# Batch 1's k and q by another queue, cast on chip, and turned six blocks a piece

## The chip, the cores and the metric

The kernel runs on one core of one Trainium2 chip. Its engines are TensorE (PE), VectorE (DVE), ScalarE (ACT), GpSimd (POOL) and SyncE (SP). PE multiplies, and turns blocks of data by a multiplication with an identity matrix; DVE, ACT and POOL work on elements; SP only issues DMAs. ACT and POOL issue DMAs too. A DMA that POOL issues can change the type on its way (fp32 in memory, bf16 on chip); one that SP issues here cannot. The two kinds run in different queues on the same 16 DMA engines: in the profile POOL's are the queue q0, "software_dynamic", and SP's are q1, "hardware_dynamic".

The metric is the device time in microseconds (us) of one execution; the median of several runs is compared.

## What is computed

Chunked attention over 4 batches, 8 heads, 768 positions of 64 elements, with 8 memory rows for each head, and then a feed-forward layer with a sine in it, over all 3072 positions:

```python
for c in range(S // 32):                       # chunks of 32 queries
    l, r = max(0, 32*c - 16), min(S, 32*c + 40)
    k_full = concat([mem_k, k[:, :, l:r]]); v_full = concat([mem_v, v[:, :, l:r]])
    a = softmax(q[:, :, 32*c:32*c + 32] @ k_full.T / sqrt(64))
    out[:, :, 32*c:32*c + 32] = a @ v_full
x = out.transpose(0, 2, 1, 3).reshape(3072, 512)
h = x @ w_in                                   # 512 x 2048
g = h + sin(alpha * h)**2 / (alpha + 1e-9)
return g @ w_out                               # 2048 x 512
```

## The kernel before

**The stages.** The work runs as a front and four passes. The front makes the attention of batch 0. Pass i makes the feed-forward layer of batch i, and, woven into it, the attention of batch i+1. The order of everything is written out by hand as strings of words, one letter and some digits each, and a method `do_<letter>` issues what a word stands for. Each engine works off its own instructions strictly in that order, so a word that waits holds up what stands behind it on the same engine.

**The feed-forward words.** The inner size 2048 is cut into 16 tiles. `b7` and `h7` multiply the two halves of tile 7 (four matmuls each, line 424) and let ACT take the sine (line 439); `q7A`, `q7V` or `q7P` square it on ACT, DVE or POOL (lines 444 and 447); `g7` makes the tile of gT on DVE from it (line 451) and frees the PSUM banks. `f9` issues nine matmuls of the second product (line 462), which has its own queue of waiting work; finished rows are copied by ACT or DVE (line 469) and written by SP (line 472).

**The attention words.** Batches 0 and 1 get their turned k and q from PE. `k2` turns piece 2 of k (a piece is a pair of heads) and `l2` piece 2 of q (`turn`, line 269); `K2V`, `L2A` copy the result out of PSUM on DVE or ACT (lines 285, 291 and 299) into kT and qT. `s61` makes the scores of blocks 6 and 1 (lines 385 and 399) and needs all pieces; `v0` multiplies block 0 by the values (line 414); `T0`, `t1`, `c6` turn the result into the next batch's x. Batches 2 and 3 get their turned k and q from DMA transposes and are not touched by the change.

**The loads.** `I7g` loads the columns of w_in for tiles 7 to 15, `I27` those for tiles 2 to 6 (line 213); `U12` loads one block of rows of w_out (line 219); `V125` loads v of batch 1, heads 2 to 4 (lines 172 and 179, two DMAs). All are POOL's, and cast on their way. At most eight of POOL's DMAs are under way: the ninth waits until the first has landed.

For batch 0 SP loads k and q in fp32, a piece at a time, into `kq_f` (line 708), and words like `a4V` cast a piece on ACT or DVE (`do_a`, line 653) into `k_bf` or `q_bf`. For batch 1 two words in pass 0, `dq108` and `dk108`, let POOL load all of q and all of k at once, cast by the DMA (`load_one`, line 155).

**The layout.** `k_bf` and `q_bf` hold 128 rows of `(head, r, d)`, with r from 0 to 5 and d from 0 to 63. A block of one head is 64 columns wide, so `turn` makes 12 transposes a piece: six for each of the two heads, the first head's into rows 0 to 63 of PSUM and the second head's into rows 64 to 127.

**gT.** The pool that holds gT has two buffers that passes use in turn.

In pass 0 the words around the pieces of batch 1 stand in this order (others left out):

```
b0 h0 I7g U69 U12 b1 h1 dq108 b4 h4 b3 h3 b6 dk108 b2 h2 h6 b5 h5 Ufg b7 U01 U56 q6P h7 U24 q7P U45 ... V158 ...
l0 l2 l3 q13P k2 Ube U9b Uef ... V125 k1 k0 l1 K1V k3 L1V L3A q14V K3A K0A V102 f9 g14 s61
```

Of the kernel before, what the change touches and what calls it, by code (L numbers as in the profile page):

```python
# [9 lines left out]
P = 128  # L10
# [4 lines left out]
BF = mybir.dt.bfloat16  # L15
F32 = mybir.dt.float32
ACTF = mybir.ActivationFunctionType
ALU = mybir.AluOpType


class Feed:
# [64 lines left out]
def kernel(  # L86
# [12 lines left out]
    nc = tc.nc  # L99
    B, H, S, D = q.shape  # L100
# [4 lines left out]
    HP = H // 2  # L105
    FT = d_ff // P
    KT = d_model // P
    NSUB = S // P
# [14 lines left out]
    ident = consts.tile([P, P], BF, name="ident")  # L123
# [17 lines left out]
    qst = q_bf[:].rearrange("p h r d -> p (h r d)").rearrange("p (t c) -> p t c", t=NSUB)  # L141
# [8 lines left out]
    inv_alpha = consts.tile([P, FT], F32, name="inv_alpha")  # L150

    def load_one(src, dst, b, h0, h1):
        nc.gpsimd.dma_start(
            dst[:, h0:h1].rearrange("p h r d -> p h (r d)"),
            src[b, h0:h1].rearrange("h (p r) d -> p h (r d)", p=P),
        )

    def load_v(b, h0, h1):  # L160
        vw = vws[b % 2][:].rearrange("p h j c -> p (h j) c")
# [107 lines left out]
    def turn(src, hp):  # L269
        bank, bs = banks.single()  # L270
        t = bank[:, 0:384].bitcast(BF).rearrange("p (r c) -> p r c", r=6)
        for r in range(6):
            for e in range(2):
                nc.tensor.transpose(
                    t[64 * e:64 * e + 64, r, :], src[:, 2 * hp + e, r, :], ident[:]
                )
# [73 lines left out]
    def normed(otv, bs):  # L350
# [5 lines left out]
            in1=rinv[:].unsqueeze(3).to_broadcast([QW, 2, HP, D]),  # L356
            op=ALU.mult,
        )
# [82 lines left out]
    def squared(t, eng):  # L441
# [3 lines left out]
        else:  # L445
            e = nc.vector if eng == "V" else nc.gpsimd
            e.tensor_tensor(out=s2[:], in0=u[:], in1=u[:], op=ALU.mult)  # L447

    def finish(t, gT):
# [53 lines left out]
    class Stage:  # L503
# [146 lines left out]
        def do_a(self, a):  # L650
            hp = int(a[0]) % HP
            dst = kq[int(a[0]) // HP]
            copier(a[1])(
                dst[:, 2 * hp:2 * hp + 2].rearrange("p h r d -> p h (r d)"), kq_f[int(a[0])][:]
            )

        def do_C(self, a):
            consts_of[a]()
# [4 lines left out]
        def do_d(self, a):  # L663
            if a == "m":
                nc.gpsimd.dma_start(memv_st[64:72].rearrange("n b h d -> n (b h) d"),
                                    mem_v.rearrange("b h n d -> n (b h) d"))
            elif a == "y":
                for bb in range(1, B):
                    if CROSSED[bb][0]:
                        nc.gpsimd.dma_start(  # L670
                            memv_st[96:104, bb],
                            mem_k[bb].rearrange("h n d -> n h d"))
            else:
                src, dst = (k, k_bf) if a[0] == "k" else (q, q_bf)
                load_one(src, dst, int(a[1]), int(a[2]), int(a[3]))

        def do_I(self, a):
            load_w_in(P * int(a[0], 17), P * int(a[1], 17))
# [21 lines left out]

    kq_f = [mlp.tile([P, 2, 6 * D], F32, name="kq_f", tag=t) for t in ("u", "s2") * 4]
    memk_f = mlp.tile([P, H, D], F32, name="memk_f", tag="o_sb", bufs=3)
    alpha_rows = mlp.tile([FT, P], F32, name="alpha_rows", tag="o_sb", bufs=3)

    def load_f(src, hp, t):
        nc.sync.dma_start(
            t[:], src[0, 2 * hp:2 * hp + 2].rearrange("h (p r) d -> p h (r d)", p=P)
        )  # L710

    load_f(k, 0, kq_f[0])
# [90 lines left out]
    def const_s():  # L803
# [6 lines left out]
    first = {}  # L810
    stage = Stage(-1, None)
    stage.tile = first
    stage.run((
# [3 lines left out]
    ))  # L817
    for i, words in enumerate(((
# [6 lines left out]
    ),(  # L825
# [5 lines left out]
    ),(  # L831
# [5 lines left out]
    ),(  # L837
# [3 lines left out]
    ))):  # L841
        stage = Stage(i, stage.nx).run(words)
    feed.take(400)

# [28 lines left out]
```

## Time and profile before

| | |
|---|---|
| median of 3 runs | 216.53 us (216.51 to 219.29) |
| span of the profiled execution, first to last instruction | 213.1 us |
| what the median has beyond that span | 3.4 us |
| PE busy | 201.7 us, 95% of the span |
| ACT, DVE, POOL busy | 143.5, 140.5, 99.8 us |
| granted TensorE clock | 1.000 throughout |
| read from memory, written | 29.66 MB, 6.29 MB |

The profiled execution's own time is not listed apart from its span; sums over the trace are made against the span, and 3.4 us are added to compare with the median. In the rows of a timeline the columns are start, length, engine, line, operation, destination and source, count, and in brackets the idle time before it and what ended that; PEq, SPq and the like are queues that issue. A row may join several instructions that follow each other.

### The profile page before, as it was taken

The numbers are of one execution on the slowest core, as the hardware profiler recorded it, in microseconds if no ns is written. First come the engines' busy times: TensorE is split into PE (matmuls) and PEld (weight loads), VectorE is DVE, ScalarE is ACT, GpSimd is POOL, SyncE is SP. The second block draws the span as 40 slices with busy tenths as digits, with TensorE's granted clock in tenths as the row PEclk, the third lists the DMA queues.
The fourth block names the chain that finished last, engine by engine and source line by source line (L and its number), as shares of the span: only waits on it lengthen the run. The fifth ranks groups of instructions, "written<-read, shape, count | busy, mean of one in ns | idle before, by whom it ended". The sixth has DMA issues, their size and how long they took to land.

```text
span 213.1 us, 4479 instructions
## 1 busy us (share of the span) xinstructions
PE 201.7 (95%) x1721; PEld 113.5 (53%) x1721; DVE 140.5 (66%) x218; ACT 143.5 (67%) x230; POOL 99.8 (47%) x140
## 2 busy tenths in 40 slices
PE   0799899999999999999999999999999999999994
PEld 0456555565455556555455555554555555554443
DVE  7598678999542749975856649898157197865011
ACT  2597898976857469977846199887846289891110
POOL 8959515688598193009991039659400023200000
PEclk9999999999999999999999999999999999999999
DMA  6999999999999999969999229989945400000312
GB/s 195 337 163 141 193 209 205 204 163 182 131 177 141 137 148 144 180 88 110 126 217 171 72 63 131 156 126 129 175 115 123 124 15 0 2 3 0 148 49 98
DMA packets 95908, 28.19 MB, mean 132 GB/s; under 512 B 84864, under 2 KB 92432, under 8 KB 95888
## 3 DMA queue, kind: packets, MB, share of 16 engines
q0 software_dynamic: 68736, 13.25, 92.3%
q1 hardware_dynamic: 26976, 14.62, 28.2%
q8 instruction: 13, 0.21, 0.4%
q14 instruction: 7, 0.06, 0.1%
q10 hardware_dynamic: 176, 0.04, 0.1%
HBM read 29.66 MB, written 6.29 MB: 169 GB/s over the span
## 4 chain that ended last, share of the span: by engine, by line
PE 71%; DVE 9%; DMA 7%; ACT 4%; issue 4%; POOL 3%; DVEq 0%; POOLq 0%; ACTq 0%
PE ps L462 38%; PE ps L424 27%; DMA memv_st<-in_mem_v_dram 4%; DVE gT L451 4%; DVE s L447 3%; DMA vw<-in_v_dram 3%; PE ps L414 3%; PE ps L385 2%; ACT u L439 2%; PE ps L366 1%; ACT s L444 1%; POOL s L447 1%; POOL vw L172 1%; DVE kT L285 1%; ACT L699 1%
## 5 line engine op out<-in xcount | busy, mean ns | idle before, releaser
L462 PE MATMUL ps<-w_out_sb,gT 128*128 128x512 bf16 (+2 forms) x400 | 89.1, 371 | 0.0
L424 PE MATMUL ps<-xT,w_in_sb 128*128 128x384 bf16 x512 | 86.0, 326 | 0.7 <-DVE gT L451 0.4
L451 DVE SCALAR_TENSOR_TENSOR gT<-s,inv_alpha,ps 128x768 bf16<-128x768 f32 x64 | 63.0, 1011 | 12.5 <-ACT s L444 5.2
L424 PEld LDWEIGHTS <-w_in_sb 128*128 128x128 bf16 x512 | 49.8, 98 | 35.4 <-issue 2.1
L439 ACT ACTIVATE u<-ps,alpha_sb 128x768 f32<-128x768 f32 x64 | 56.6, 895 | 16.8 <-PE ps L424 14.3
L462 PEld LDWEIGHTS <-gT 128*128 128x128 bf16 x400 | 36.6, 98 | 37.9 <-DVE gT L451 0.2
L447 POOL TENSOR_TENSOR s<-u 128x768 f32<-128x768 f32 x11 | 17.4, 1582 | 69.7 <-ACT u L439 69.7
L399 ACT ACTIVATE pt<-ps,biasm 128x256 bf16<-128x256 f32 x72 | 27.2, 489 | 10.5 <-PE ps L385 10.5
L469 DVE COPY o_sb<-ps 128x512 f32<-128x512 f32 (+1 forms) x15 | 10.1, 678 | 28.3 <-PE ps L462 26.4
L447 DVE TENSOR_TENSOR s<-u 128x768 f32<-128x768 f32 x23 | 21.9, 953 | 7.8 <-ACT u L439 7.8
L444 ACT ACTIVATE s<-u 128x768 f32<-128x768 f32 x30 | 25.0, 841 | 0.5
L354 DVE TENSOR_TENSOR x_blk<-ps,rinv 96x512 bf16<-96x512 f32 x32 | 22.0, 687 | 1.1
L469 ACT COPY o_sb<-ps 128x512 f32<-128x512 f32 (+1 forms) x10 | 5.6, 562 | 21.6 <-PE ps L462 21.6
L172 POOL DMA_DIRECT2D vw<-in_v_dram x13 | 12.9, 994 | 7.9 <-PE ps L366 5.4
L353 DVE RECIPROCAL rinv<-ps 96x8 f32<-96x8 f32 x32 | 6.4, 200 | 13.5 <-PE ps L414 12.7
L179 POOL DMA_DIRECT2D vw<-in_v_dram x13 | 12.7, 976 | 0.0
L238 POOL DMA_DIRECT2D kst<-in_k_dram x16 | 12.2, 760 | 1.1 <-DMA vw<-in_v_dram 0.8
L232 POOL DMA_DIRECT2D kst<-in_k_dram x16 | 11.3, 708 | 2.3 <-DMA vw<-in_v_dram 1.6
L369 ACT COPY xT<-ps 128x384 bf16<-128x384 bf16 x12 | 5.6, 496 | 8.2 <-PE ps L366 8.2
L245 POOL DMA_DIRECT2D q_bf<-in_q_dram x12 | 10.7, 912 | 0.0
L414 PEld LDWEIGHTS <-pt 128*128 128x128 bf16 x192 | 8.2, 97 | 4.2 <-ACT pt L399 0.3
L414 PE MATMUL ps<-vw,pt 128*128 128x65 bf16 x192 | 8.9, 193 | 0.0
(81 smaller groups left out, 131.4 us busy)
## 6 DMA issues: line engine op xcount, KB each, us to landing
out_dram<-o_sb SPq DMA_DIRECT2D x23, 256.0 KB, 2.3
kq_f<-in_k_dram SPq DMA_DIRECT2D x4, 384.0 KB, 6.5
kq_f<-in_q_dram SPq DMA_DIRECT2D x4, 384.0 KB, 6.0
q_bf<-in_q_dram POOLq DMA_DIRECT2D x12, 128.0 KB, 6.7
w_in_sb<-in_moe_w_in_dram POOLq DMA_DIRECT2D x1, 1152.0 KB, 12.6
vw<-in_v_dram POOLq DMA_DIRECT2D x7, 128.0 KB, 6.7
vw<-in_v_dram POOLq DMA_DIRECT2D x8, 112.0 KB, 7.4
kst<-in_k_dram POOLq DMA_DIRECT2D x14, 64.0 KB, 5.1
```

Of the source, the lines that this page charges most:

```text
L172: nc.gpsimd.dma_start(vw[0:64, lo:c1, 0:D], win(vflat, a, n, 64))
L179: nc.gpsimd.dma_start(vw[72:128, c0:hi, 0:D], win(vflat, base + QW * c0 + 48, hi - c0, 56))
L354: nc.vector.tensor_tensor(out=x_blk[:].rearrange("p g e d -> p e g d"), in0=otv[0:QW, :, :, 0:D], in1=rinv[:].unsqueeze(3).to_broadcast([Q ...
L399: nc.scalar.activation(pt[:, 0:H * QW].rearrange("p (g e c) -> p g e c", g=2, e=4)[:, :, :, 32 * m:32 * m + 32], sc[:, :, 0:4 * QW].rearra ...
L414: nc.tensor.matmul(otv[:, e, hp, :], pt[:, QW * i:QW * i + P], vws[b % 2][:, 2 * hp + e, j, 0:D + 1],)
L424: nc.tensor.matmul(t["hT"][:, hf, 0:HALF], w_in_sb[:, kt, P * t["ft"]:P * t["ft"] + P], t["xT"][:, kt, HALF * hf:HALF * hf + HALF], start= ...
L439: nc.scalar.activation(t["u"][:], t["hT"][:, :, 0:HALF], ACTF.Sin, scale=alpha_sb[:, ft:ft + 1])
L444: nc.scalar.activation(s2[:], u[:], ACTF.Square)
L447: e.tensor_tensor(out=s2[:], in0=u[:], in1=u[:], op=ALU.mult)
L451: nc.vector.scalar_tensor_tensor(out=gT[:, ft, :].rearrange("p (e c) -> p e c", e=2), in0=t["s2"][:], scalar=inv_alpha[:, ft:ft + 1], in1= ...
L462: nc.tensor.matmul(o[:, c0:c1], gT[:, ft, P * s:P * s + P], w_out_sb[:, ft, c0:c1], start=(ft == 0), stop=(ft == FT - 1),)
L469: copier(state["engines"][state["o"] % len(state["engines"])])(o_sb[:, c0:c1], o[:, c0:c1])
```

## The change

For batch 1, k and q are loaded by SP in fp32, in eight DMAs of one piece each, as batch 0's are. They go into `kq_1`, a tile of the gT pool that takes the buffer which pass 1's gT takes after it; pass 0's gT has the other. Two words `jqP0123` and `jkP0123` stand where `dq108` and `dk108` stood; each sets a few elements of the tile to zero on POOL, and SP's DMAs wait for that. Both zeroings stand on POOL's queue next to each other, behind the DMA of `U12`. Eight new words cast the pieces, all on POOL: `a4P a6P` right behind `q7P`'s squaring; `a7P a2P` between `U45` and `V158`; `a1P a0P a5P a3P` between `Uef` and `V125` (pieces 0 to 3 are k's, 4 to 7 are q's). POOL issues two DMAs fewer.

`k_bf` and `q_bf` now hold `(pair, r, head, d)`, so the blocks of the two heads of a pair lie side by side and `turn` makes six transposes of 128 columns a piece, for batch 0's pieces as well. The casts of batch 0 stay on ACT and DVE and write to the new order. All other words stand as they stood. Line numbers of the new kernel are some 20 to 30 higher.

```diff
-    k_bf = consts.tile([P, H, 6, D], BF, name="k_bf")
-    q_bf = consts.tile([P, H, 6, D], BF, name="q_bf")
+    k_bf = consts.tile([P, HP, 6, 2, D], BF, name="k_bf")
+    q_bf = consts.tile([P, HP, 6, 2, D], BF, name="q_bf")
...
         for r in range(6):
-            for e in range(2):
-                nc.tensor.transpose(
-                    t[64 * e:64 * e + 64, r, :], src[:, 2 * hp + e, r, :], ident[:]
-                )
+            nc.tensor.transpose(
+                t[:, r, :], src[:, hp, r].rearrange("p e d -> p (e d)"), ident[:]
+            )
...
         def do_a(self, a):
             hp = int(a[0]) % HP
             dst = kq[int(a[0]) // HP]
-            copier(a[1])(
-                dst[:, 2 * hp:2 * hp + 2].rearrange("p h r d -> p h (r d)"), kq_f[int(a[0])][:]
-            )
+            copy = nc.gpsimd.tensor_copy if a[1] == "P" else copier(a[1])
+            copy(dst[:, hp].rearrange("p r e d -> p e r d"),
+                 kq_f[int(a[0])].rearrange("p e (r d) -> p e r d", r=6))
...
+        def do_j(self, a):
+            x0 = 0 if a[0] == "k" else HP
+            hps = [int(c) for c in a[2:]]
+            eng = {"V": nc.vector, "P": nc.gpsimd}[a[1]]
+            for hp in hps:
+                kq_f[x0 + hp] = kq_1[:, x0 + hp]
+            eng.memset(kq_1[0:1, x0 + hps[0]:x0 + hps[-1] + 1, 0, 0:1], 0.0)
+            for hp in hps:
+                load_f(k if x0 == 0 else q, hp, kq_f[x0 + hp], 1)
...
+    kq_1 = gp.tile([P, 2 * HP, 2, 6 * D], F32, name="kq_1", tag="gT")
...
-    def load_f(src, hp, t):
+    def load_f(src, hp, t, b=0):
         nc.sync.dma_start(
-            t[:], src[0, 2 * hp:2 * hp + 2].rearrange("h (p r) d -> p h (r d)", p=P)
+            t, src[b, 2 * hp:2 * hp + 2].rearrange("h (p r) d -> p h (r d)", p=P)
         )
```

Pass 0's words in the two places, before and after:

```
before  b1 h1 dq108 q1A b4 h4 b3 g0 h3 b6 g1 dk108 q4V
after   b1 h1 jqP0123 q1A b4 h4 b3 g0 h3 b6 g1 jkP0123 q4V

before  q7P g6 h10 b9 q10A g5 h9 U45 b8 h8 g7 g10 q8A q9V V158
after   q7P g6 h10 b9 q10A g5 h9 a4P a6P U45 b8 h8 g7 g10 q8A q9V a7P a2P V158

before  Ube b15 U9b g11 Uef g13 K2V h15 b12 q15V h12 q12A b14 g15 f7 h14 V125 k1 k0
after   Ube b15 U9b g11 Uef g13 K2V h15 b12 q15V h12 q12A b14 g15 f7 h14 a1P a0P a5P a3P V125 k1 k0
```

More of the change, by code (lines that the diff above doesn't have):

```diff
@@ L18 @@
 ALU = mybir.AluOpType
+FRONT = (
[3 rows of a table added]
+)
+PASSES = ((
[5 rows of a table added]
+), (
[5 rows of a table added]
+), (
[5 rows of a table added]
+), (
[3 rows of a table added]
+))
 class Feed:
@@ L138 @@
     kst = consts.tile([P, NJ, H * D], BF, name="kst")
-    k_bf = consts.tile([P, H, 6, D], BF, name="k_bf")
-    q_bf = consts.tile([P, H, 6, D], BF, name="q_bf")
-    qst = q_bf[:].rearrange("p h r d -> p (h r d)").rearrange("p (t c) -> p t c", t=NSUB)
+    k_bf = consts.tile([P, HP, 6, 2, D], BF, name="k_bf")
+    q_bf = consts.tile([P, HP, 6, 2, D], BF, name="q_bf")
+    qst = q_bf[:].rearrange("p g r e d -> p (g r e d)").rearrange("p (t c) -> p t c", t=NSUB)
     NK = NM * sum(not CROSSED[b][0] for b in range(B))
@@ L150 @@
     inv_alpha = consts.tile([P, FT], F32, name="inv_alpha")
[L154 to L157, printed above, removed]
-        )
     def load_v(b, h0, h1):
@@ L272, in turn @@
         for r in range(6):
-            for e in range(2):
-                nc.tensor.transpose(
-                    t[64 * e:64 * e + 64, r, :], src[:, 2 * hp + e, r, :], ident[:]
-                )
+            nc.tensor.transpose(
+                t[:, r, :], src[:, hp, r].rearrange("p e d -> p (e d)"), ident[:]
+            )
         return t, bs
@@ L652, in do_a @@
             dst = kq[int(a[0]) // HP]
-            copier(a[1])(
-                dst[:, 2 * hp:2 * hp + 2].rearrange("p h r d -> p h (r d)"), kq_f[int(a[0])][:]
-            )
+            copy = nc.gpsimd.tensor_copy if a[1] == "P" else copier(a[1])
+            copy(dst[:, hp].rearrange("p r e d -> p e r d"),
+                 kq_f[int(a[0])].rearrange("p e (r d) -> p e r d", r=6))
         def do_C(self, a):
@@ L672, in do_d @@
                             mem_k[bb].rearrange("h n d -> n h d"))
-            else:
-                src, dst = (k, k_bf) if a[0] == "k" else (q, q_bf)
-                load_one(src, dst, int(a[1]), int(a[2]), int(a[3]))
+        def do_j(self, a):
[7 more added lines that the diff above has]
+                load_f(k if x0 == 0 else q, hp, kq_f[x0 + hp], 1)
         def do_I(self, a):
@@ L699, in warm @@
         nc.scalar.activation(tiny[:], zeros[0:1, 0:1], func)
-    kq_f = [mlp.tile([P, 2, 6 * D], F32, name="kq_f", tag=t) for t in ("u", "s2") * 4]
+    kq_f = [mlp.tile([P, 2, 6 * D], F32, name="kq_f", tag=t)[:] for t in ("u", "s2") * 4]
+    kq_1 = gp.tile([P, 2 * HP, 2, 6 * D], F32, name="kq_1", tag="gT")
     memk_f = mlp.tile([P, H, D], F32, name="memk_f", tag="o_sb", bufs=3)
     alpha_rows = mlp.tile([FT, P], F32, name="alpha_rows", tag="o_sb", bufs=3)
-    def load_f(src, hp, t):
+    def load_f(src, hp, t, b=0):
         nc.sync.dma_start(
-            t[:], src[0, 2 * hp:2 * hp + 2].rearrange("h (p r) d -> p h (r d)", p=P)
+            t, src[b, 2 * hp:2 * hp + 2].rearrange("h (p r) d -> p h (r d)", p=P)
         )
@@ L812 @@
     stage.tile = first
-    stage.run((
[3 rows of a table removed]
-    ))
-    for i, words in enumerate(((
[6 rows of a table removed]
-    ),(
[5 rows of a table removed]
-    ),(
[5 rows of a table removed]
-    ),(
[3 rows of a table removed]
-    ))):
+    stage.run(FRONT)
+    for i, words in enumerate(PASSES):
         stage = Stage(i, stage.nx).run(words)
```

43 rows, old and new, of tables (FRONT, PASSES, stage) are left out of this document.

## The prediction

> **What bounds the kernel now.** I read the page first, then PE's rows in order of time around the pieces of batch 1, then POOL's rows, then the DMA queues by stretch.
>
> ```profile
> PE 201.7 (95%) x1721; PEld 113.5 (53%) x1721; DVE 140.5 (66%) x218; ACT 143.5 (67%) x230; POOL 99.8 (47%) x140
> ...
> 22.29 0.42 PE L344 MATMUL ps<-vw,pt 128*128 128x65 bf16 x8 [0.25 <-DMA vw<-in_v_dram]
> 24.81 17.62 PE L424 MATMUL ps<-xT,w_in_sb 128*128 128x384 bf16 x104
> ...
> 42.36 1.29 PE L274 MATMUL ps<-ident,q_bf 128*64 128x128 bf16 x36
> 43.46 0.53 PE L274 MATMUL ps<-ident,k_bf 128*64 128x128 bf16 x12
> 44.10 3.46 PE L424 MATMUL ps<-xT,w_in_sb 128*128 128x384 bf16 x20
> ...
> 48.94 0.81 PE L424 MATMUL ps<-xT,w_in_sb 128*128 128x384 bf16 x4
> 49.68 0.86 PE L274 MATMUL ps<-ident,k_bf 128*64 128x128 bf16 x24
> 50.37 0.50 PE L274 MATMUL ps<-ident,q_bf 128*64 128x128 bf16 x12
> 50.71 0.50 PE L274 MATMUL ps<-ident,k_bf 128*64 128x128 bf16 x12
> 51.14 2.17 PE L462 MATMUL ps<-w_out_sb,gT 128*128 128x512 bf16 x9
> 53.52 0.51 PE L385 MATMUL ps<-qT,kT 64*128 64x96 bf16 x16 [0.20 <-DVE kT L291]
> ...
> L424 PE MATMUL ps<-xT,w_in_sb 128*128 128x384 bf16 x512 | 86.0, 326 | 0.7 <-DVE gT L451 0.4
> ```
>
> PE is the bound: 95% busy on the page, and from 24.81 us on its rows follow each other without a hole worth naming. So work taken from PE in pass 0 is a gain, and every wait put into PE's queue there is a loss at full price. The pieces are turned in two groups, at 42.36 (l0 l2 l3, then k2) and at 49.68 (k1 k0, l1, k3). The scores that need all of them start at 53.52, 0.20 us late already.
>
> ```profile
> 18.03 2.27 POOL L213 DMA_DIRECT2D w_in_sb<-in_moe_w_in_dram  x3
> 21.61 0.91 POOL L155 DMA_DIRECT2D q_bf<-in_q_dram  x1
> 22.50 0.90 POOL L155 DMA_DIRECT2D k_bf<-in_k_dram  x1
> 36.64 1.48 POOL L447 TENSOR_TENSOR s<-u 128x768 f32<-128x768 f32 x1
> 38.06 0.59 POOL L219 DMA_DIRECT2D w_out_sb<-in_moe_w_out_dram  x1
> 38.65 0.98 POOL L172 DMA_DIRECT2D vw<-in_v_dram  x1
> 39.62 1.02 POOL L179 DMA_DIRECT2D vw<-in_v_dram  x1
> 42.99 0.95 DVE L447 TENSOR_TENSOR s<-u 128x768 f32<-128x768 f32 x1
> 43.45 1.82 POOL L447 TENSOR_TENSOR s<-u 128x768 f32<-128x768 f32 x1 [2.81 <-ACT u L439]
> 45.22 2.12 POOL L219 DMA_DIRECT2D w_out_sb<-in_moe_w_out_dram  x3
> 47.33 0.97 POOL L172 DMA_DIRECT2D vw<-in_v_dram  x1
> ```
>
> POOL is 47% busy over all, but not here: from 36.64 to 47.33 its only hole is the 2.81 us in which it waits for tile 13's sine. This is the stretch into which all eight casts go.
>
> **The transposes.** PE's rows give its pace. L424's 104 end at 24.81 + 17.62 = 42.43; the last of them takes 0.326, and the first leaves PE to the next after 0.166 (3.46 less one latency is 19 steps), so PE was free for the next matmul at 42.27. It came at 44.10: the 48 of the first group cost 1.83 us, 38 ns each. By the same steps PE is free at 48.94 + 4 x 0.166 = 49.6 and L462 goes on at 51.14: the second group costs 1.54 us, 32 ns each. For the new form (a full 128 columns) the trace has no row; the nearest are full-width blocks of 96 rows:
>
> ```profile
> 23.79 0.68 PE L366 MATMUL ps<-ident,x_blk 96*128 96x96 bf16 x12 [0.49 <-DVE x_blk L354]
> ```
>
> Less one latency (0.21 us) that is 11 in 0.47 us, 43 ns each at 96 columns; by columns 56 ns at 128. So 24 cost 1.34 us where 48 cost 1.83 and 1.54: a gain of 0.5 and 0.2 us, 0.7 in all if PE has nothing else to wait for. The count halves, the time hardly does, since the old blocks are half as wide. The Trainium skill, TensorEngine Tiling (Array Packing), Key Properties, says that column tiles work in parallel and that a change of the tiling mode drains the array. The 32 to 38 ns agree with the first. The Trainium skill, TensorE: Matmul & The Clock Gate, Back-to-back issue gap, gives about 81 ns for a weight load with a 128-column matmul; by that 24 would cost 1.94 us, a loss of 0.1 to 0.4 us a group. I keep 56 ns by the row. The same edit in the front I cost at nothing: PE waits there for loads as late as 22.29 us, and the casts of batch 0 move the same elements. If that cover went, eight pieces at some 0.1 us would gain 0.8.
>
> **The loads.** Each of the eight pieces lands in fp32 by the other queue. SP issues nothing between the front and the first rows of output, so nothing is queued behind these DMAs there. POOL loses 1.81 us of issue at 21.61, which ends no wait of PE. What changes is who shares the 16 engines with the w_in columns that tiles 2 to 6 and 7 to 15 wait for.
>
> ```profile
> w_in_sb<-in_moe_w_in_dram POOLq DMA_DIRECT2D x1, 1152.0 KB, 12.6
> ...
> w_in_sb<-in_moe_w_in_dram POOLq DMA_DIRECT2D x1, 640.0 KB, 7.9
> ...
> 0.76 0.45 SPq L708 DMA_DIRECT2D kq_f<-in_k_dram  x1
> ...
> q1 hardware_dynamic: 52, 0.08, 38.2%
> ...
> q0 software_dynamic: 666, 0.97, 112.4%
> ...
> q0 software_dynamic: 641, 1.11, 113.0%
> ...
> q1 hardware_dynamic: 254, 0.37, 102.1%
> ...
> q1 hardware_dynamic: 198, 0.29, 95.3%
> q0 software_dynamic: 195, 0.01, 25.0%
> ```
>
> The queue rows are those of the stretches 1.5 to 2.5, 21.7 to 26.7, 26.7 to 32, 9 to 10 and 10 to 11 us, in this order. Issued at about 18.8 and 19.5 (three in 2.27 us from 18.03), the two parts of w_in land at 26.7 and 32.1. PE opens its third tile after 16 matmuls, at 24.81 + 16 x 0.169 = 27.5, and its eighth after 56, at 34.3: the margins are 0.8 and 2.2 us. Before, k and q stood behind w_in in one queue. Now SP's packets come from some 22.9 us on (issue at 21.7, and 1.2 us to the first packet, an estimate from 0.76 and the 52 packets by 2.5 us) beside them. In the front, where both queues had work (10 to 11 us), they got 198 and 195 packets: turn by turn. A packet of SP's alone takes 16/254 = 63 ns of an engine; one of w_in 5.0 x 16/666 = 120 ns, later 132. The first part has at most 512/16 = 32 packets an engine left (one for each of 128 rows and 4 blocks): between 0 and 2.0 us late, 1.5 by the share still to come, a wait of 0.7. The second has 32 as well, 2.0 us more: 35.6 against 34.3 + 0.7, a wait of 0.6 to 0.8. Sum 1.5 us, between 0 and 2.5.
>
> The pieces land in SP's order q0 to q3, k0 to k3. k2 is the seventh: 112 packets an engine, alone 7.1 us, beside a w_in packet at each turn 21.8, so between 30 and 44.7 us, more likely 43 to 44 since after w_in the partners are the shorter ones of w_out.
>
> **The casts.** No row shows POOL casting fp32. Rows beside it:
>
> ```profile
> L447 POOL TENSOR_TENSOR s<-u 128x768 f32<-128x768 f32 x11 | 17.4, 1582 | 69.7 <-ACT u L439 69.7
> L195 POOL COPY vw<-memv_st 8x512 bf16<-8x512 bf16 x8 | 5.1, 676 | 0.0
> L760 POOL COPY mind<-asum 128x768 bf16<-128x768 bf16 x1 | 0.8, 815 | 0.0
> ```
>
> A copy of the same 768 elements is 0.815 us, a copy in runs of 64 by elements 676 x 768/512 = 1.01, two fp32 inputs 1.58. One input and runs of 64: I take 0.9, with 0.68 and 1.58 as ends. Then POOL's queue after the change, starting from the end of q7P's squaring (38.12) and the 1.5 us by which PE is late:
>
> 39.6; a4P and a6P 1.8, U45 0.59: 42.0; a7P 0.9, a wait of some 0.5 for k2, a2P 0.9: 44.3; V158 2.0: 46.3; q13P 1.65 (between 1.48 and 1.82): 47.95; three DMAs of w_out 2.12: 50.1; a1P, a0P, a5P, a3P 3.6: 53.7.
>
> PE's first group is covered: l0, l2, l3 would be due at 43.8 and k2 near 44.9, and their casts are ready at 42.9 and 44.3. The second group is not. k3 can be turned at 53.7, and its six end at 54.0, where k3's twelve let the next matmul start at 51.14. Behind it in PE's queue stand f9, the scores and all the rest. f9 (2.2 us) covers the copies of k3 to kT as before, and the 0.20 us wait of the scores stays or goes. The time after that is PE's, with no hole to take up a delay: the end moves by 54.0 - 51.14 = 2.9 us. The 1.5 us of w_in lie inside it, as does the gain of the transposes.
>
> V125 and V102 are issued behind a3P, 6.4 us later than at 47.33; the last of them at some 56.6.
>
> ```profile
> 60.95 0.41 PE L414 MATMUL ps<-vw,pt 128*128 128x65 bf16 x8
> ...
> vw<-in_v_dram POOLq DMA_DIRECT2D x8, 112.0 KB, 7.4
> ```
>
> It lands at 64.0 and the values need it at 60.95 + 2.9 = 63.85: nothing, or up to 1.5 us; I take nothing, as the queue ahead of it is shorter then. q13P comes 2.7 us later, so g13 on DVE and the words behind it do too; PE's order puts them beside the wait for k3.
>
> Sum: 213.1 + 2.9 = 216.0 of span, and 3.4 outside it: **219.4 us**. With a cast of 0.82 us, w_in 0.8 us late and no wait for k2 the same sum ends k3 at 52.0 (217.4); with 1.01, 1.9, 1.2 and 1.82 for q13P at 56.1 (221.5).
>
> **The rivals.** *POOL keeps up, and PE gains (not slower).* Without a delay by w_in the queue from 38.12 holds 0.59 + 2.0 + 1.48 + 2.12 = 6.2 us and eight casts before 50.7 plus the little that PE has then gained: it decides at a cast of 0.78 us. Below that the casts hide, and the 0.7 us of the transposes are left, less the 0.20 us: 216.0. For it speaks the plain copy of 0.815, just above; against it the margins of w_in. Chance 0.22.
>
> *A dear cast.* At the price of two inputs, 1.58, the same queue ends at 39.6 + 12.6 + 6.4 = 58.6, 7.8 us late: 224.3. The two squarings with start times above took 1.48 and 1.82 us, the long one beside DVE's of 42.99, so POOL does lose time beside DVE. The Trainium skill, GPSIMD Engine Reference, Specifications, says that POOL shares its SBUF interfaces with DVE and suffers from instructions with two SBUF inputs, which is what DVE's squarings are. The 1.82 us agree; no row shows it for a cast. Chance 0.13.
>
> *SP's packets go first.* All 128 packets an engine, 8.1 us, ahead of w_in: its first part at 34.8, PE waits 7.3 us at the third tile, POOL's queue starts at 45.4 and k3's turn ends 8.2 us late: 224.7. In 9 to 10 us SP's queue had 254 packets and the other almost none, but that one's had only begun to come, and the even count a microsecond later speaks against it. Chance 0.10.
>
> **How the numbers follow.** The forecast has 0.55, its own range 217.4 to 221.5. About 2%, 4.3 us, is what a measurement of this kernel can tell from no change; slower by that is above 220.9. The two dear rivals (0.23) lie there and 0.08 of the forecast: 0.31. Faster by it nothing forecasts: 0.03 for what I don't see. Within: 0.66. The range 215.5 to 224.4 leaves out half of the two dear rivals and 0.05 below.
>
> **What would show it.** Right: POOL's casts near 0.9 us, back to back, a3P ending between 52 and 55; PE idle ahead of k0, l1 and k3 and for 0.5 to 1 us each at the third and eighth tile, released by w_in's DMA. Wrong: a cast under 0.78 us; w_in landing where it did; SP's eight DMAs over by 32 us; transposes not near 56 ns; or waits that open later, at the first values or in pass 1.

## The result and the profile after

| | before | after |
|---|---|---|
| median, 4 runs each | 216.52 us (214.79 to 219.29) | 224.88 us (223.5 to 226.3) |
| span of the profiled execution | 213.1 us | 222.1 us |
| mean granted TensorE clock | 1.000 | 0.985 |

The changed kernel is slower: a ratio of 1.0405 with a 95% interval of 1.0335 to 1.0476. The forecast was 219.4 us and its range ended at 224.4. Ratios here leave disturbed runs out (seven of ten in one kernel below) and are taken against runs of before on the same chip, so they can differ from the quotient of two medians; the profiled run of the first ordered kernel below was such a run (352.71 us), and its trace is not used.

From the page of after: busy times, the clock in 40 slices, and the chain that ended last, by line.

```profile
PE 206.6 (93%) x1625; PEld 116.2 (52%) x1625; DVE 142.9 (64%) x218; ACT 143.4 (65%) x230; POOL 104.7 (47%) x148
...
PEclk9999999985999999999999999999999999999999
...
PE ps L483 34%; PE ps L445 26%; DMA kq<-in_k_dram 9%; DMA memv_st<-in_mem_v_dram 4%; PE ps L435 2%; SPq L737 2%; PE ps L406 2%; DVE gT L472 1%; DVE s L468 1%; ACT s L465 1%; DMA xT<-x_blk 1%; POOL w_in_sb L235 1%; SPq L654 1%; PE ps L387 1%; POOL vw L194 1%
```

A DMA of k is now on the chain with 9% of the span, and in one place the clock falls to half. Where the time went stands in PE's rows of after in order of time (line 445 was 424, 295 was 274, 483 was 462, 406 was 385):

```profile
26.09 9.47 PE L445 MATMUL ps<-xT,w_in_sb 128*128 128x384 bf16 x56
36.25 4.07 PE L445 MATMUL ps<-xT,w_in_sb 128*128 128x384 bf16 x24 [0.69 <-DMA w_in_sb<-in_moe_w_in_dram]
...
45.14 1.42 PE L295 MATMUL ps<-ident,q_bf 128*128 128x128 bf16 x18 [0.58 <-DVE gT L472]
49.09 0.82 PE L295 MATMUL ps<-ident,k_bf 128*128 128x128 bf16 x6 [2.53 <-POOL k_bf L675]
49.71 6.08 PE L445 MATMUL ps<-xT,w_in_sb 128*128 128x384 bf16 x20
...
58.78 0.50 PE L295 MATMUL ps<-ident,k_bf 128*128 128x128 bf16 x6
59.12 2.39 PE L483 MATMUL ps<-w_out_sb,gT 128*128 128x512 bf16 x9
61.58 0.52 PE L406 MATMUL ps<-qT,kT 64*128 64x96 bf16 x16
```

Set against the rows of before, PE is late by 1.95 us at the eighth tile (36.25 against 24.81 + 56 x 0.169 = 34.3), by 2.78 at the first turn (45.14 against 42.36), by 5.63 at k2 (49.09 against 43.46), by 7.98 behind the last turn (59.12 against 51.14) and by 8.06 at the scores (61.58 against 53.52). Nearly all of the 8.4 us between the medians is there before batch 1's scores. The other 0.9 us of the 9.0 between the spans comes later; 0.7 of it is one wait of PE for a DMA that makes x.

POOL's rows of after, in order of time:

```profile
40.17 1.59 POOL L675 CAST q_bf<-kq 128x768 bf16<-128x768 f32 x2
42.31 0.84 POOL L675 CAST q_bf<-kq 128x768 bf16<-128x768 f32 x1
48.21 0.83 POOL L675 CAST k_bf<-kq 128x768 bf16<-128x768 f32 x1 [5.06 <-DMA kq<-in_k_dram]
50.98 1.48 POOL L468 TENSOR_TENSOR s<-u 128x768 f32<-128x768 f32 x1
...
54.50 2.35 POOL L675 CAST k_bf<-kq 128x768 bf16<-128x768 f32 x2
...
57.57 0.82 POOL L675 CAST k_bf<-kq 128x768 bf16<-128x768 f32 x1
```

A cast takes 0.80 to 0.84 us. But POOL stands for 5.06 us with the cast of k2, since k2 has not landed. Behind it in POOL's queue are V158 and the squaring of tile 13, which ran at 43.45 before and runs at 50.98 now, then U, and then the second four casts, whose last ends at 58.39. k3 is turned 0.39 us after that. So POOL's queue, held by one DMA, ends just ahead of k3. PE has no idle time of its own in front of k3, though: its rows from 49.71 on, at half clock, get there at about the same time. What PE would have waited for at full clock is shown further down (the half clock). DVE's rows of after:

```profile
42.21 1.76 DVE L468 TENSOR_TENSOR s<-u 128x768 f32<-128x768 f32 x1
52.49 1.01 DVE L472 SCALAR_TENSOR_TENSOR gT<-s,inv_alpha,ps 128x768 bf16<-128x768 f32 x1 [4.50 <-POOL s L468]
54.48 1.69 DVE L468 TENSOR_TENSOR s<-u 128x768 f32<-128x768 f32 x1
```

DVE waits 4.50 us for tile 13, which POOL squares. And two of DVE's own squarings, 0.95 us in the profile of before, take 1.76 and 1.69 us; beside the first stands POOL's cast of 42.31, beside the second the casts of 54.50.

Why k2 is late, from SP's issues (a joined row of four), the chain, and the DMA queues in the stretches 25 to 26, 26 to 27 and 30 to 36 us of after (packets, MB, share of 16 engines):

```profile
22.60 2.63 SPq L737 DMA_DIRECT2D kq<-in_q_dram  x4
25.32 9.19 SPq L737 DMA_DIRECT2D kq<-in_k_dram  x4
28.24 19.85 DMA kq<-in_k_dram
...
q0 software_dynamic: 150, 0.19, 118.7%
...
q0 software_dynamic: 98, 0.17, 94.4%
q1 hardware_dynamic: 31, 0.05, 15.7%
...
q0 software_dynamic: 481, 0.82, 73.2%
q1 hardware_dynamic: 483, 0.70, 37.7%
...
w_in_sb<-in_moe_w_in_dram POOLq DMA_DIRECT2D x1, 1152.0 KB, 15.9
```

The two queues take turns packet by packet (483 beside 481), as forecast. But SP has no packet at all before 26.2 us, 3.6 us after its first issue at 22.60. In all seven kernels here that load this way and whose trace can be read, it is 3.5 to 4.2 us. k2 is the seventh of eight and lands at 28.24 + 19.85 = 48.09. The last row: the 1152 KB of w_in need 15.9 us to land where they needed 12.6 (15.1 to 16.7 in the seven kernels, 12.6 to 14.5 in those that load as before).

### The profile page after: what moved, and what is told of

Read it like the earlier page. It is cut to its first block, busy times and chain, and to the rows that moved or that the text cites. A ratio compares the mean times of both kernels' runs of the same rounds, so it can differ in the third digit from the quotient of the medians.

```text
span 222.1 us, 4308 instructions
## 1 busy us (share of the span) xinstructions
PE 206.6 (93%) x1625; PEld 116.2 (52%) x1625; DVE 142.9 (64%) x218; ACT 143.4 (65%) x230; POOL 104.7 (47%) x148
## 4 chain that ended last, share of the span: by engine, by line
PE 66%; DMA 14%; POOL 5%; DVE 4%; SPq 3%; issue 3%; ACT 2%; POOLq 0%; DVEq 0%
PE ps L483 34%; PE ps L445 26%; DMA kq<-in_k_dram 9%; DMA memv_st<-in_mem_v_dram 4%; PE ps L435 2%; SPq L737 2%; PE ps L406 2%; DVE gT L472 1%; DVE s L468 1%; ACT s L465 1%; DMA xT<-x_blk 1%; POOL w_in_sb L235 1%; SPq L654 1%; PE ps L387 1%; POOL vw L194 1%
## 5 line engine op out<-in xcount | busy, mean ns | idle before, releaser
L445 PE MATMUL ps<-xT,w_in_sb 128*128 128x384 bf16 x512 | 88.9, 332 | 1.9 <-DMA xT<-x_blk 0.7
L460 ACT ACTIVATE u<-ps,alpha_sb 128x768 f32<-128x768 f32 x64 | 56.6, 894 | 24.3 <-PE ps L445 21.8
L445 PEld LDWEIGHTS <-w_in_sb 128*128 128x128 bf16 x512 | 50.5, 100 | 38.7 <-issue 6.0
L468 DVE TENSOR_TENSOR s<-u 128x768 f32<-128x768 f32 x23 | 23.4, 1019 | 8.6 <-ACT u L460 8.6
L254 POOL DMA_DIRECT2D kst<-in_k_dram x16 | 12.3, 770 | 0.3 <-DMA vw<-in_v_dram 0.3
L260 POOL DMA_DIRECT2D kst<-in_k_dram x16 | 11.7, 734 | 0.1
L295 PE MATMUL ps<-ident,k_bf 128*128 128x128 bf16 x48 | 5.5, 276 | 3.8 <-POOL k_bf L675 2.5
## 6 DMA issues: line engine op xcount, KB each, us to landing
w_in_sb<-in_moe_w_in_dram POOLq DMA_DIRECT2D x1, 1152.0 KB, 15.9
```

Source lines behind the costliest of these rows:

```text
L445: nc.tensor.matmul(t["hT"][:, hf, 0:HALF], w_in_sb[:, kt, P * t["ft"]:P * t["ft"] + P], t["xT"][:, kt, HALF * hf:HALF * hf + HALF], start= ...
L460: nc.scalar.activation(t["u"][:], t["hT"][:, :, 0:HALF], ACTF.Sin, scale=alpha_sb[:, ft:ft + 1])
```

## The experiments

**The order of the loads.** Theory: the largest part is k2's place in SP's queue. The same kernel with SP's loads in the order in which the casts need them, one zeroing for all; run twice, the second time for its trace.

```diff
-b1 h1 jqP0123 q1A b4 h4 b3 g0 h3 b6 g1 jkP0123 q4V        (SP: q0 q1 q2 q3 k0 k1 k2 k3)
+b1 h1 jP46721053 q1A b4 h4 b3 g0 h3 b6 g1 q4V             (SP: q0 q2 q3 k2 k1 k0 q1 k3)
```

> The changed kernel, with SP's eight DMAs in the order in which the casts need them (q0 q2 q3 k2 k1 k0 q1 k3), all behind one zeroing; nothing else differs. Theory (k2, the seventh in SP's queue, lands at 48.1 us and holds POOL 5.1 us, then PE 2.5 us, and PE's clock falls after it): k2 is now fourth and lands near 38 to 41 us, POOL's wait for it is gone, PE's granted clock stays at 1.00 between 42 and 60 us, and the time falls by 4 to 6 us to 218 to 221. Rival (POOL's queue of casts is what delays PE, whatever lands when): POOL's casts of the second group still end after PE wants them, and the time falls by less than 2 us, to 223 or more.

> The kernel with SP's loads in the order of need again, for its trace: the first profile of it had a granted clock of 0.57 from end to end and says nothing of the order. Theory (k2's landing held POOL and PE): k2 lands before 43 us, POOL's squaring of tile 13 starts near 47 to 48 instead of 51, the first scores of batch 1 start near 57 instead of 61.6, 218.5 to 220. What is left against the kernel before is then POOL's queue of casts and w_in's late columns. Rival (the gain comes from elsewhere, such as a quicker front): the scores start at 60 or later.

Measured: 219.97 us, ratio 1.0198 (1.0149 to 1.0247), and 220.61 us, ratio 1.0233 (1.0134 to 1.0331). Rows of DVE, POOL and PE of the second run, in order of time:

```profile
42.12 2.52 DVE L468 TENSOR_TENSOR s<-u 128x768 f32<-128x768 f32 x1
42.99 0.83 POOL L675 CAST k_bf<-kq 128x768 bf16<-128x768 f32 x1
45.76 1.48 POOL L468 TENSOR_TENSOR s<-u 128x768 f32<-128x768 f32 x1
...
51.08 2.15 DVE L468 TENSOR_TENSOR s<-u 128x768 f32<-128x768 f32 x1
51.59 0.82 POOL L675 CAST k_bf<-kq 128x768 bf16<-128x768 f32 x1
...
55.66 0.50 PE L295 MATMUL ps<-ident,k_bf 128*128 128x128 bf16 x6
58.45 0.51 PE L406 MATMUL ps<-qT,kT 64*128 64x96 bf16 x16 [0.35 <-DVE kT L312]
```

POOL waits for no piece, tile 13 is squared at 45.76 instead of 50.98, and the clock is 1.000. About half of the loss, 4.3 to 4.9 us by the medians, was k2's late landing; the other half stays. POOL's queue alone does not make it: the last cast ends at 52.41 us, and k3 is turned at 55.66, 3.25 us later. Before that PE waits 1.34, 0.36 and 0.87 us for DVE's gT. Three of DVE's squarings took 2.52, 1.46 and 2.15 us, 3.28 more than three of 0.95; the first and the third stood beside POOL's casts, the second beside POOL's squaring of tile 13.

**What stood behind k2.** The changed kernel with the loads as they were, but the cast of k2 behind tile 13's squaring, so that only the turn of k2 waits for the load.

```diff
-a7P a2P V158 b11 ... q13P k2
+a7P V158 b11 ... q13P a2P k2
```

> The changed kernel with POOL's cast of k2 moved behind V158 and the squaring of tile 13; SP's order of loads as in the changed kernel. Theory (the late k2 does its harm by what is queued behind its cast on POOL, the squaring of tile 13 above all, and the clock is hidden): k2 still lands near 48, PE still waits for it to about 49, but tile 13 is squared by 46 to 47, DVE does not wait 4.5 us for it, and the time falls by 1.5 to 3 us to 222 to 223. Rival (PE's own wait for k2's transposes and its half clock are the cost): less than 1 us.

Measured: 222.74 us, ratio 1.0318 (1.0239 to 1.0398). Rows of PE, DVE and POOL:

```profile
48.71 0.82 PE L295 MATMUL ps<-ident,k_bf 128*128 128x128 bf16 x6 [2.25 <-POOL k_bf L675]
...
52.94 0.97 DVE L468 TENSOR_TENSOR s<-u 128x768 f32<-128x768 f32 x1 [2.08 <-ACT u L460]
53.04 1.56 POOL L675 CAST k_bf<-kq 128x768 bf16<-128x768 f32 x1
```

Taking V158 and the squaring out from behind the wait gives back 2.1 us by the medians, though the intervals of the two ratios still overlap (1.0335 against 1.0398); PE's own wait for k2 stays, 2.25 us. Here it was a cast that lost: 1.56 us beside a squaring of DVE that took 0.97.

**The loads alone.** The ordered kernel without its eight casts; batch 1's attention is computed from batch 0's k and q.

```diff
-a4P a6P U45 ... a7P a2P V158 ... a1P a0P a5P a3P V125
+U45 ... V158 ... V125
```

> The changed kernel with SP's eight loads in the order of need and with none of the eight casts: k_bf and q_bf keep batch 0's pieces, so batch 1's attention is computed from the wrong k and q; loads, layout, turns and all other work stay. Theory (the loads cost PE a wait for w_in of about 1 us at the third or eighth tile, some 0.5 to 1.5 us in all, and the other 2.5 to 3 us of the ordered kernel's loss are POOL's casts): 216.0 to 217.2 us, a ratio of 1.003 to 1.010, DVE's squarings at 0.95 us, scores near 54 to 55 us. Rival 1 (the sharing of the DMA engines is most of the loss, the casts little): 218.5 us and more, waits for w_in of 2 us and more. Rival 2 (the loads are hidden, all of the loss is POOL's): 215.5, a ratio up to 1.002, no wait for w_in above 0.3 us.

Measured: 217.71 us, ratio 1.0120 (1.0081 to 1.0158). Rows of PE and DVE:

```profile
28.37 6.67 PE L445 MATMUL ps<-xT,w_in_sb 128*128 128x384 bf16 x40 [1.12 <-DMA w_in_sb<-in_moe_w_in_dram]
36.17 4.08 PE L445 MATMUL ps<-xT,w_in_sb 128*128 128x384 bf16 x24 [1.12 <-DVE gT L472]
42.13 0.95 DVE L468 TENSOR_TENSOR s<-u 128x768 f32<-128x768 f32 x1
...
55.50 0.51 PE L406 MATMUL ps<-qT,kT 64*128 64x96 bf16 x16
```

More than the theory's 217.2, less than the first rival's 218.5. The scores start 2.0 us late and two waits make 2.24 us. The second is put down to DVE; but the same wait at the same place, 36.17 us, is w_in's in the ordered kernel (1.06 us), and 36.25 is where it ended in the changed kernel. In the seven kernels that load this way this wait ends between 34.62 and 36.71 us, in five of them between 36.16 and 36.45. The first wait is not SP's doing alone: the kernel of the last experiment, which loads as before, has 1.37 us of it. DVE's squaring is back at 0.95 us. The profiled run was the longest of six (219.31 us); its span is 4.4 us longer than before's, and behind the scores PE waits 0.38 us for w_out and 1.0 us for x.

**The casts alone.** The kernel before with eight copies of 128 x 768 zeros into a tile that nothing reads, on POOL, at the casts' places.

```diff
-h9 U45 ... q9V V158 ... h14 V125
+h9 y4 y6 U45 ... q9V y7 y2 V158 ... h14 y1 y0 y5 y3 V125
+        def do_y(self, a):
+            nc.gpsimd.tensor_copy(scratch[:, int(a)]..., zeros[:, 0:384]...)
```

> The kernel before, with eight copies of 128x768 bf16 zeros on POOL at the places of the eight new casts, written to a tile that nobody reads; loads, layout and transposes as before. It prices POOL's queue alone. The prediction's sum (queue from 38.12 us: 6.2 us and eight copies of about 0.82, at most 1.7 us behind PE's 50.7; here nobody waits for the copies themselves, only for the squaring of tile 13 and for v behind them): copies of 0.80 to 0.85 us, tile 13's squaring 1 to 2 us later, and 216.5 to 217.5. Rival (the copies take the time from DVE's and POOL's common work): 218 or more.

Measured: 218.18 us, ratio 1.0118 (1.0072 to 1.0164). Rows of DVE and PE:

```profile
40.39 2.52 DVE L447 TENSOR_TENSOR s<-u 128x768 f32<-128x768 f32 x1
44.08 1.45 PE L274 MATMUL ps<-ident,q_bf 128*64 128x128 bf16 x36 [1.35 <-DVE gT L451]
44.87 1.47 DVE L447 TENSOR_TENSOR s<-u 128x768 f32<-128x768 f32 x1
49.36 1.38 DVE L447 TENSOR_TENSOR s<-u 128x768 f32<-128x768 f32 x1
...
55.96 0.51 PE L385 MATMUL ps<-qT,kT 64*128 64x96 bf16 x16 [0.22 <-DVE kT L291]
```

Copies that wait for no data cost 1.2%. Tile 13's squaring on POOL comes only 0.58 us later than in before (44.03), but DVE's squarings grow to 1.38 to 2.52 us (the 1.47 beside POOL's squaring of tile 13, the others beside copies); 2.52 is 0.95 and two copies of 0.79. The three take 2.5 us more than at 0.95 each, and the scores are 2.4 us late. The profiled run was the longest of the four (220.82 us): behind the scores PE waits another 3.1 us for turned q of a later batch, which it does not in before. So the scores of this trace price the copies, and its end does not. With the loads' 1.0120 this makes 1.012 x 1.0118 = 1.024, and the ordered kernel, which has both, measured 1.0198 and 1.0233.

**Whose time is taken.** Four kernels test whether a POOL instruction and a squaring of DVE exclude each other. The first two move the eight copies: in front of tile 6's squaring, where POOL waits for data in the kernel before, and behind V102.

```diff
-U01 U56 q6P
+U01 U56 y0 y1 y2 y3 y4 y5 y6 y7 q6P          (first)
-K3A K0A V102 f9
+K3A K0A V102 y0 y1 y2 y3 y4 y5 y6 y7 f9      (second)
```

> The kernel before with the eight POOL copies of zeros all in the 6.6 us in which POOL waits before it squares tile 6 (27.6 to 34.2 us). Theory 1 (a copy on POOL slows a DVE instruction with two SBUF inputs beside it, 0.95 to 1.4 to 2.5 us): the DVE squarings of that stretch (two or three) take 1.4 us or more instead of 0.95; 0.5 to 1.5 us of that may come through, 216 to 217. Theory 2 (only what is queued behind the copies on POOL counts): the squarings stay at 0.95 us and the time at 215 to 216.

> The kernel before with the eight POOL copies of zeros behind the loads of v, where no squaring is queued behind them on POOL and DVE squares nothing for some 20 us. Both theories of the copies' cost (POOL's queue, DVE slowed): no change, 214.5 to 216. Rival (POOL's extra 6.5 us cost wherever they stand, through the loads of k behind them): 217 or more.

Measured: 217.28 us, ratio 1.0068 (1.0025 to 1.0111), and 219.70 us, ratio 1.0092 (1.0020 to 1.0164). In the first the copies start at 30.01 and run into the squarings: tile 6's on POOL comes at 37.63 instead of 34.18, one of DVE's beside the copies takes 1.53 us, and PE waits 1.36 us for DVE. Its first matmul of line 424 also comes 0.94 us later than before's, and PE waits 0.68 us for w_in, so this trace does not price the copies alone. The second kernel's ten runs lie between 215.98 and 221.08 us, the profiled one at 220.35. Rows of the second, of POOL, DVE and PE:

```profile
52.13 6.93 POOL L658 COPY scratch<-zeros 128x768 bf16<-128x768 bf16 x8
53.35 4.26 DVE L447 TENSOR_TENSOR s<-u 128x768 f32<-128x768 f32 x1
58.00 0.51 PE L385 MATMUL ps<-qT,kT 64*128 64x96 bf16 x16 [3.52 <-DVE kT L291]
```

The expectation that DVE squares nothing there was wrong: tile 14's squaring (`q14V`) stands at that place. It took 4.26 us, its own 0.95 and the rest of one copy and four more; then it ran between the sixth copy and the seventh, which took 1.54 us. PE waited 3.52 us for the copies of kT behind it. In the third kernel ACT squares tile 14, behind its own copies of kT.

```diff
-L3A q14V K3A K0A V102 y0 ... y7
+L3A K3A K0A q14A V102 y0 ... y7
```

> The kernel before with the eight POOL copies of zeros late, as in the last run, but with DVE's one squaring beside them (tile 14) given to ACT, behind its copies of k. Theory (in that run DVE's squaring of 0.95 us took 4.26 beside the copies, since an instruction of DVE with two inputs from SBUF and a copy on POOL do not run together; PE then waited 3.5 us): with no such squaring in the stretch PE's wait at the first scores is under 1 us, DVE's copies out of PSUM keep their 0.26, 0.85 and 0.95 us beside POOL's, and the time is 215 to 217. Rival (POOL's extra 6.5 us cost by the loads behind them): a wait of 3 us or more stays, somewhere, and 218 or more.

Rows of PE's scores and of one copy of DVE:

```profile
53.33 0.51 PE L385 MATMUL ps<-qT,kT 64*128 64x96 bf16 x16
...
56.43 1.89 DVE L188 COPY vw<-memv_st 8x4096 bf16<-8x4096 bf16 x1
```

The wait is gone and the scores start at 53.33, 0.19 us earlier than before, with POOL's copies from 51.03 to 57.23. DVE's copies out of PSUM and its product with a PSUM operand keep their times beside them (0.25, 0.95 and 1.02 us). The copy of the second row, from SBUF to SBUF, does not: it takes 1.22 us in before and 1.89 here, where it starts 0.02 us behind the last of POOL's copies. So it is not only squarings that wait. The whole time did not follow, though: ten runs between 216.69 (the profiled one) and 225.54, median 219.78, ratio 1.0120 (1.0075 to 1.0165). That is the time that the rival named (218 or more), and no gain over the kernel with `q14V` in its place: by the times, eight copies behind V102 cost as much with no squaring in their way. In the profiled run PE waits 1.7 us for a DMA that makes x of a later batch; before has no such wait. What makes the other runs longer stays open.

In the fourth, the ordered kernel casts a piece by two additions of zero, half a piece each, two inputs instead of one.

```diff
-            copy(to, of)
+            for e in range(2):
+                nc.gpsimd.tensor_tensor(out=to[:, e], in0=of[:, e], in1=z, op=ALU.add)
```

> The kernel with SP's loads in the order of need, but each POOL cast done as two additions of zeros (two inputs, half a piece each), near 1.5 us a piece instead of 0.83. Theory 1 (POOL's copies hold DVE's squarings up, 2.52, 1.46 and 2.15 us against 0.95; additions with two inputs hold them up less, as POOL's squarings did in the kernel before, where DVE kept 0.95 us): DVE's squarings between 40 and 55 us are near 0.95 us again, and although POOL's queue is 5 us longer the time rises by less than 2 us, 219.5 to 222. Theory 2 (POOL's queue is what counts): 223 to 226. Rival (any POOL work on all rows holds DVE up): squarings of 2 us and more, 223 or more.

Measured: 228.67 us, ratio 1.0588 (1.0513 to 1.0663). Rows of DVE:

```profile
43.98 4.81 DVE L468 TENSOR_TENSOR s<-u 128x768 f32<-128x768 f32 x1
52.35 5.25 DVE L468 TENSOR_TENSOR s<-u 128x768 f32<-128x768 f32 x1
```

POOL's form does not matter to the squarings: one input, two inputs, zeros or data, they wait. The 5.25 us hold five additions. The 4.81 us hold more than additions: less its own 0.95, the squaring begins some 1.0 us after the end of the last of them (46.86), behind a DMA issue of POOL, and why is open. The 1.0588 is not all DVE's: PE also waits 1.17 and 1.22 us for POOL's casts themselves. The Trainium skill, SBUF — State Buffer, SBUF: two separate sides, says that GpSimd and a VectorE instruction with two SBUF inputs share a pair of ports under an exclusive lock: the one that starts first keeps it for its whole instruction, and the other is blocked. The trace agrees that they are blocked rather than slowed (0.95 + 0.81 = 1.76, and 2.52, 4.26). It does not settle who is first: DVE's record starts 0.10 us ahead of POOL's at 42.21 in the changed kernel and DVE loses; it starts 0.10 us ahead at 52.94 in the kernel with q13P first and POOL loses.

**The casts on DVE.** The ordered kernel with its casts on DVE, and in exchange tiles 9 and 11 squared on POOL.

```diff
-a4P a6P U45 ... q9V a7P a2P V158 ... k2 q11V ... a1P a0P a5P a3P V125
+a4V a6V U45 ... q9P a7V a2V V158 ... k2 q11P ... a1V a0V a5V a3V V125
```

> The changed kernel with SP's loads in the order of need, the eight casts of batch 1 on DVE instead of POOL (a4V and so on, at the same places) and the squarings of tiles 9 and 11 on POOL instead of DVE. Theory (what is left of the loss is POOL's and DVE's turns at each other's expense, and DVE has no idle time from 37 to 52 us): the casts take 0.6 to 0.7 us, no squaring of DVE is over 1.1 us beside a cast, but DVE has 5.2 - 1.9 = 3.3 us more to do in that stretch, so the scores start 2 to 3 us after 53.5 and the time is 218 to 220 us, about that of the ordered kernel. Rival 1 (the exclusion alone is the loss, DVE's own time is not): 216 to 217. Rival 2 (DVE's casts hold POOL's squarings up as well): POOL's squarings of tiles 9, 11 and 13 above 2 us, 221 us and more.

Measured: 224.95 us, ratio 1.0431 (1.0391 to 1.0470). Rows of DVE and PE:

```profile
49.53 1.94 DVE L472 SCALAR_TENSOR_TENSOR gT<-s,inv_alpha,ps 128x768 bf16<-128x768 f32 x2 [2.46 <-POOL s L468]
58.09 0.71 PE L295 MATMUL ps<-ident,q_bf 128*128 128x128 bf16 x6 [1.77 <-DVE gT L472]
```

All theories missed. No squaring is stretched (POOL's two from 46.61 take 2.89 us together), yet the time is worse. DVE's casts took 0.55 to 1.03 us, and only one of them stood beside a squaring of POOL, for 0.25 us, so the second rival was hardly tested. Tiles 13 and 11 now follow each other on POOL, DVE waits 2.46 us for them, and then the four casts stand ahead of gT's tiles in DVE's queue, for which PE waits 1.77 us. Part of this loss is the exchange of the two squarings, not the casts. Neither POOL nor DVE has room for the casts here; ACT was not tried.

**The half clock.** Another suspect is PE itself: the twenty matmuls at 49.71 took 6.08 us where before they took 3.46. Twelve matmuls on zeros, whose result nothing reads, fill PE's wait ahead of k2.

```diff
-L2A q13P k2
+L2A q13P z12 k2
```

> The changed kernel with 12 matmuls of zeros (128x512, results unused, 2.6 us at full clock) on PE ahead of k2's transposes, where PE waits for POOL's cast of k2. Theory (PE's wait of 2.5 us lets the clock fall to half from about 48 to 55 us, which alone costs 2.6 us): PE is busy through the wait, the clock stays at 1.00, the 20 matmuls of tiles 13 to 15 behind k2 take 3.3 to 3.5 us instead of 6.1, and the time falls by 2 to 3 us to 222 to 223. Rival (the half clock is hidden by other waits, so that only k2's landing counts): no change, 224.5 to 225.5; or slower by up to 2.6 us if the zeros are in the way.

Measured: 223.47 us, ratio 1.0378 (1.0346 to 1.0411). Rows of PE:

```profile
49.52 2.76 PE L445 MATMUL ps<-xT,w_in_sb 128*128 128x384 bf16 x16
...
53.52 0.81 PE L445 MATMUL ps<-xT,w_in_sb 128*128 128x384 bf16 x4 [1.24 <-DVE gT L472]
...
61.34 0.51 PE L406 MATMUL ps<-qT,kT 64*128 64x96 bf16 x16 [0.35 <-DVE kT L312]
```

The clock stays full, and sixteen matmuls take 2.76 us. Then PE waits for DVE, which waits for tile 13 from POOL, and the scores start 0.24 us earlier. So the slow matmuls filled time in which PE would have waited anyway, for gT behind tile 13, which stands behind k2's cast on POOL. The medians are 1.4 us apart, but the two ratios' intervals overlap.

**The transposes and the layout.** The kernel before, batch 0's pieces laid out by pair and turned by six transposes; the rest as it was.

```diff
-self.piece["k" + a] = turn(k_bf, int(a))
+self.piece["k" + a] = turn(k_bf, int(a), self.b == 0)     (q alike)
```

> The kernel before, with batch 0's pieces alone laid out pair by pair and turned by six transposes; batch 1's loads and its twelve transposes a piece stay as they were. Theory (the first matmul of pass 0 starts 1.3 us later in the changed kernel because PE, with fewer transposes, stays at half clock to about 17 us instead of 9): the front ends 0.8 to 1.5 us later than before and the time is 217.3 to 218. Rival 1 (the later front is chance in the first loads, not the change): 216 to 217, no difference. Rival 2 (fewer transposes help the front): 215 to 216.

Measured: 215.24 us over ten runs, ratio 1.0005 (0.9976 to 1.0034): no difference. The first matmul of line 445 at 26.09 in the changed kernel, 1.28 us later than before, is then not the layout's; the ordered, the loads' and the DVE-cast kernels, with the same front, have it at 25.32, 24.48 and 25.97, and the two kernels with copies in front of q6P and behind V102, with the old front, at 25.75 and 26.00.

## Why the prediction was wrong

**The step that failed** is the landing of k2: "between 30 and 44.7 us, more likely 43 to 44", with "a wait of some 0.5 for k2" on POOL. It landed at 48.09 and POOL waited 5.06 us. The transfer itself was near its upper bound: 112 packets an engine, each beside one of the other queue, were put at 21.8 us at most, and 26.2 + 21.8 = 48.0 (the likelier 43 to 44 had 20 to 21 us). What was wrong is the start, "from some 22.9 us on", taken from a lone first DMA on idle engines; here SP's first packet came at 26.2 us, 3.3 us later. Of these, 0.9 us are the issue (22.60 instead of 21.7, since the front was later), and 2.4 us the time from issue to first packet, 3.6 instead of 1.2. The other queue filled the engines then (95 to 119% in each us from 22 to 26); that this held SP back is likely, but no run tests it. The bound of 44.7 hung on the same start, so the range had no room for it. Put 48.09 into the prediction's own queue for POOL: cast to 49.0, V158 to 51.0, tile 13 to 52.5, U to 54.6, four casts of 0.82 to 57.9, k3 turned by 58.2, 7.1 us late; 213.1 + 7.1 + 3.4 = 223.6, against 224.88. The ordered kernel shows the other side: without the wait, 219.97 and 220.61, where the prediction had 219.4.

**Right for a partly wrong reason.** That 219.4 came so near is in part luck. Its path went from POOL's last cast, at 53.7, to k3, at 54.0; in the ordered kernel the last cast ended at 52.41, and k3 was turned at 55.66, behind waits for DVE. It had no price for DVE's squarings. The sharing stood among the rivals, but with POOL as the one that loses, as a dear cast of 1.58 us. The casts took 0.80 to 0.84 (0.9 forecast), apart from those that met a squaring first; the loser was mostly DVE, and eight copies alone cost 1.2%, with PE waiting for DVE ahead of the scores. (That copies behind V102 cost as much with no squaring beside them is not explained.) In the ordered kernel the scores come 4.9 us late (58.45 against 53.52) where the sum had 2.9, and in the one with the loads alone 2.0: the difference of these two, 2.9 us, is the casts', of which the sum saw only POOL's queue.

**Right.** PE is the bound, and delays ahead of the scores come out at the end at about full price (8.06 us at the scores, 8.4 in the medians). The transposes: 24 in the second group from 57.78 to 59.12 are 1.34 us, as worked out from 96-column blocks at 56 ns for 128 columns. The 81 ns that the prediction quotes from the Trainium skill (TensorE: Matmul & The Clock Gate, Back-to-back issue gap), by which 24 would take 1.94, do not hold here. The front cost nothing. The queues take turns; SP's packets do not go first. w_in: forecast at 35.6 us for its second part and 1.5 us of wait in all, measured near 36.2, with PE 1.95 us late at the eighth tile. Its first part, with 0.7 us of that forecast, made no wait in the changed kernel; where there is one (0.2 to 1.1 us in five kernels that load this way), two kernels that load as before have it too (0.68 and 1.37 us). The later loads of v end no wait of PE: none of its waits behind 62 us is for v.

**Not foreseen.** Where the wait for k2 is, the clock halves; it hid behind the wait for tile 13. And PE waits 0.3 to 1.7 us for the DMA that makes x in later passes in eight of the twelve other profiles, and 1.4 and 3.1 us for turned q in two more; in before it has neither. In all but one of the twelve the end is 0.4 to 3.4 us further behind before's than the scores are. This was seen and not tested.

By ratios the whole is: loads 1.2%, casts 1.2%, and the place of k2 in SP's queue some 1.7 to 2.1% (1.0405 over 1.0233 and 1.0198).

## What to carry to other kernels

When a load moves to another queue, date its first packet by one that started beside like traffic, not by a DMA that ran alone (here 3.5 to 4.2 us after the issue instead of 1.1), and issue the pieces in the order in which they are used; then look at what stands behind the first waiting instruction on its engine. Before giving POOL work, look for DVE instructions with two SBUF inputs in the same stretch, and for its copies from SBUF to SBUF: they and POOL's work add up instead of overlapping. Halving the number of instructions is worth little where their width doubles.

## What the runs showed of the hardware

- POOL's instructions that read SBUF and DVE's squarings ran one after the other: 0.95 us became 1.76 beside one cast, 2.52 beside two, 4.26 beside the rest of one copy and four more, 5.25 beside five additions. Which goes next was not always the same: a waiting squaring was passed by a second cast in the ordered kernel (42.12 us) and by four copies behind V102, but got in after the first of two casts in the changed kernel (54.48 us), and the second then took 1.57. DVE's instructions with a PSUM operand were not held up.
- DVE's copy from SBUF to SBUF (`vw<-memv_st`, 1.22 us) and POOL get in each other's way too: it took 1.89 us behind a copy of POOL, and in ten of the thirteen profiles, before among them, a DMA issue of POOL beside it took 1.0 to 1.7 us instead of 0.7, and ended 0.24 to 0.28 us after the copy.
- Beside a busy POOL queue SP's was slow to start and slow to issue: 3.5 to 4.2 us from the first issue to the first packet in seven kernels (1.1 us in the front of before), and 9.19 us for four issues that in the front of before take about 0.45 us apiece.
- The granted TensorE clock was 0.50 in 49 to 55 us of the changed kernel, behind PE's wait of 2.53 us, in 58 to 64 us of the kernel with additions, behind one of 3.96, and in 59 to 60 us of the kernel with the casts on DVE, behind one of only 1.77. Behind the 3.52 us of the kernel with the copies behind V102 it stayed 1.000, so the length of the wait alone doesn't decide it here.
